# Polysketch attention into a SwiGLU block on one core: the first batch's third token block made of split products behind the first two blocks

## Chip, core and metric

One NeuronCore of a Trainium2 chip. The metric is device microseconds of one execution, from before the first instruction to after the last; three executions of the kernel before took 278.92, 278.66 and 278.62 us (median 278.66). The engines are TensorE (PE, with its weight loads, PEld), VectorE (DVE), ScalarE (ACT), GpSimd (POOL), and SyncE (SP), which issues the DMAs.

## What is computed

```python
# attention: batch 4, heads 4, 1088 tokens, head_dim 32, r = 8
def phi(x):
    a = np.einsum('rd,bhsd->bhsr', S1, x)
    b = np.einsum('rd,bhsd->bhsr', S2, x)
    return np.einsum('bhsi,bhsj->bhsij', a, b).reshape(*x.shape[:-1], r * r)
q_p, k_p = (phi(q), phi(k))
kv = np.einsum('bhsf,bhsd->bhfd', k_p, v)
z = np.sum(k_p, axis=2)
num = np.einsum('bhsf,bhfd->bhsd', q_p, kv)
den = np.einsum('bhsf,bhf->bhs', q_p, z)[..., None] + 1e-06
attn = num / den
# bridge: (B,H,S,D) -> (B*S, H*D), 4352 tokens of 128
x = np.ascontiguousarray(attn.transpose(0, 2, 1, 3)).reshape(B * S, H * D)
# d_model 128, d_ff 1536
g = x @ w_gate
silu = g * (1.0 / (1.0 + np.exp(-g)))
out = (silu * (x @ w_val)) @ w_out
```

Inputs and output are float32, except that S1, S2 and the three weights arrive as float64 words, which the kernel narrows to FP32 itself.

## The kernel before

**Blocks and units.** The 4352 tokens are ten blocks: batch 0 has blocks 0, 1 and 2 of 384, 384 and 320 tokens; from block 3 on (`HEAD`, the first of `line`) a block has 480 tokens, the last 384. d_ff is cut into 12 chunks of 128. A *unit* (i, j) makes hidden chunk j of block i: a gate and a value product with the 128 x 128 weights of chunk j, a SiLU on ScalarE, and a product of both on VectorE. A *down* (i, j) multiplies the hidden chunk by a 128 x 128 piece of w_out and accumulates in one PSUM bank per block; after a block's twelfth down, `store` transposes it on VectorE and SP writes it out with four or eight DMAs.

**Two kinds of products.** In blocks 0 to 2, `unit` (L1026) uses plain FP32 products (L1034). A plain FP32 product shows as two PE records. From block 3 on a unit is made of parts: `start_unit` (L990) multiplies a difference of the weights (wd) with a difference of the tokens (xd), L997, and ScalarE scales both PSUM banks in place (L1000); `finish_unit` (L1002) adds two products per bank on top, w1 by x1 (L1010) and wb by x0 (L1011); then SiLU (L1013) and a VectorE product (L1018). These six matmuls are of type fp32r and show as one record each. The tokens' parts x1, x0, xd are made by `cut_tokens` (L873), one ScalarE and two VectorE or POOL operations; the weights' parts w1, low, wb, wd by `cut_weights` (L840), for each of four groups of three chunks, in four steps: ScalarE, an engine for the subtraction, ScalarE, the engine again. Some downs of later blocks are made of parts too (L1074 to L1077).

**Banks.** PSUM has eight banks: g0, g1, g2, acc (0 to 3) and two pairs a (4, 5) and b (6, 7). A plain unit takes two of the first four in turn, a down's sum one of g1, g2, acc. `pair()` gives the least lately used free pair out of (0, 1), (4, 5) and (6, 7). A unit of parts holds its pair from its start until the VectorE product is recorded.

**Attention of the batches.** Batch 0 is done by itself at the beginning, block by block (`divide`, L539, writes the tokens xT). For the others a generator, `attentions()` (L615), is asked for its next piece by `parts_of(n)`: turning keys and queries on VectorE (L327, L578), key products (L354), key features (L377), their sums on POOL (`feature_sums`, L543), key-value products (L388), the spread of these by transposes and six small DMAs (`spread_out`), query sketches (L342), the query step (L745 to L762: a dot product, a sum, an addition, a reciprocal, a multiplication, and three times features and a transpose), and the numerators (L780), which ScalarE and VectorE copy into xT.

**The order.** It is written out by hand: each engine runs its instructions in the order in which the program records them. After the first units of blocks 0 and 1, the loop at L1300 runs over 30 plain units of blocks 0, 1 and 2; between them stand the narrowing of weights (`part`), the loads of batch 1, and from the 18th unit on one down per unit, a piece of attention, and the cutting of weights. The loop from L1345 then runs the downs that are left, three at a time, with pieces of attention between, until the numerators of batch 1 are done and block 3's tokens are cut; `start_unit(0)` and the last two downs follow. The main loop over the units of blocks 3 to 9 (L1376) starts the next unit, finishes this one, and makes a down when more than five are waiting.

Of the kernel before, what the change touches and what calls it, by code (L numbers as in the profile page):

```python
# [19 lines left out]
def kernel(  # L20
# [162 lines left out]
    coming += [("wo", i) for i in range(len(pieces["wo"]))]  # L183
# [126 lines left out]
    NH = 27  # L310
# [231 lines left out]

    def feature_sums(phk):  # L543

        rows = phk[:].rearrange("p c h i j -> p c (h i j)")
        s = apool.tile([P, 4, H * F], FP32, tag="zs", name="zs")
        add = lambda o, a, b: nc.gpsimd.tensor_tensor(out=o, in0=a, in1=b, op=ALU.add)

        def last():
            add(s[:, 0, :], s[:, 0, :], s[:, 1, :])  # L550
            add(s[:, 0, :], s[:, 0, :], rows[:, 8, :])

        return s[:, 0, :], [
            lambda: add(s[:, 0:2, :], rows[:, 0:2, :], rows[:, 4:6, :]),
            lambda: add(s[:, 2:4, :], rows[:, 2:4, :], rows[:, 6:8, :]),
            lambda: add(s[:, 0:2, :], s[:, 0:2, :], s[:, 2:4, :]),
            last,
        ]
# [56 lines left out]
    def attentions():  # L615
# [4 lines left out]
        yield from turn_queries(1)  # L620
        hold("a")
        kp = wide("a")
# [8 lines left out]
        for i, (c0, c1) in enumerate(kpieces):  # L631
            nc.scalar.copy(ka[:, H * c0 : H * c1, :], sketch(kp, i)[:, :, 0, :])
        phk = apool.tile([P, NC, H, R, R], FP32, tag="phk", name="phk")
        for n, (i, c0, c1) in enumerate(((0, 0, 3), (0, 3, 5), (1, 5, 7), (1, 7, 9))):
            first = H * (c0 - kpieces[i][0])
            kb = sketch(kp, i)[:, first : first + H * (c1 - c0), 1, :]
            key_features(phk, (ka[:, H * c0 : H * c1, :], kb), c0, c1)
            if n == 3:
                release("a")
            if n % 3 != 1:  # L640
                yield
        zs, sums = feature_sums(phk)
        for f in sums:
            f()
        yield from turn_keys(2)
        kvz = wide("a")
        key_values(kvz[:, 0, 0:F], phk, 0, NC)
        value_sums(kvz[:, 0, :], zs)
        kab, kcopies = sketched(wide("b"), key_products, 2, "kab2")
        fold(kvz[:, 0, :])  # L650
        spread = spread_out(1, kvz[:, 0, :])
        hold("a", "b")
        yield
        qab, copies = sketched(wide("a"), query_sketches, 3, "qab")
        run_copies(copies, 2)
        yield
        run_copies(kcopies, 2)
        release("a", "b")
# [3 lines left out]
        yield  # L662
        yield
        numerators(1, spread, (wide("a"), wide("b")))
# [159 lines left out]
    def homes(w):  # L824


        if w is wv:
            for c in range(4):
                yield [
                    stage.tile([P, 3, P], F32R, tag=tag, name=name, bufs=6)[:]  # L830
                    for tag, name in (("exp", "w1"), ("man", "wb"), (("exp", "man")[c % 2], "wd"))
                ]
        else:
            big = lambda pool, tag, bufs: pool.tile([P, 2, 3, P], F32R, tag=tag, name="g" + tag, bufs=bufs)
            for c in range(2):
                t = [big(stage, "raw", NRAW), big(stage, "raw", NRAW), big(apool, "phq", 2)]
                for k in range(2):
                    yield [x[:, k] for x in t]

    def cut_weights(w, lows, engine):  # L840

        rows = [], [], [], []
        sub = dict(op=ALU.subtract)
        for c, (w1, wb, wd) in enumerate(homes(w)):
            src = w[:, 3 * c : 3 * c + 3, :]
            low = lows[c]
            w_parts[id(w), c] = (w1, wb, wd)
            fine = dict(out=wd, in0=whole(w1), in1=whole(wb), **sub), engine.tensor_tensor
            if engine is nc.vector:
                fine = dict(  # L850
                    out=wd, in0=low, scalar=-BETA, in1=whole(w1), op0=ALU.mult, op1=ALU.add
                ), engine.scalar_tensor_tensor
            for row, f, args in zip(
                rows,
                (nc.scalar.activation, engine.tensor_tensor, nc.scalar.activation, fine[1]),
                (
                    dict(out=w1, in_=src, func=AF.Copy, scale=CUT),
                    dict(out=low, in0=src, in1=whole(w1), **sub),
                    dict(out=wb, in_=low, func=AF.Copy, scale=BETA),
                    fine[0],  # L860
                ),
            ):
                row.append((f, args))
        return rows

    def take(steps, n):

        for _ in range(n):
            if steps:
                f, args = steps.pop(0)  # L870
                f(**args)

    def cut_tokens(i, engine=nc.gpsimd):  # L873
# [21 lines left out]
        first, second = (difference, low) if engine is nc.vector else (low, difference)  # L895
# [94 lines left out]
    def start_unit(y):  # L990

        i, j = line[y // NCH], y % NCH
        n = blocks[i][1]
        xd = x_parts[i][2][:, 0:n]
        ps = sums_of[y] = pair(y)[:, :, 0:n]
# [6 lines left out]
    def finish_unit(y):  # L1002
        i, j = line[y // NCH], y % NCH
        n = blocks[i][1]
        x1, x0, _ = (x[:, 0:n] for x in x_parts[i])
        ps = sums_of.pop(y)
# [14 lines left out]
        let_go(y)  # L1021
# [4 lines left out]
    def unit(i, j, late=False, between=(None, None)):  # L1026
# [3 lines left out]
        g, u = bank(), bank()  # L1030
# [29 lines left out]

    def down(y=None):
# [3 lines left out]
        if j == 0:  # L1065
            acc[i] = bank("g1" if i == 1 else "g2" if i in line[2::2] else "acc")
# [3 lines left out]
        sides = dict(start=(j == 0), stop=(j == NCH - 1))  # L1070
# [12 lines left out]
        if i != LAST:  # L1083
            hidden.pop((i, j))
            slots.append(slot_of[i, j])
        if j == NCH - 1:
            if mine:
                put_together(y, i, n)
            else:
                store(i, n)  # L1090
# [153 lines left out]
    begun = [False]  # L1244

    def parts_of(n):

        for _ in range(n):
            if ahead[0] not in ("pe", "end"):
                ahead[0] = next(att, "end")  # L1250
                begun[0] |= ahead[0] == "first"
# [36 lines left out]

    w = ("wg", "wv")

    parts = {}
    for z, p in enumerate(both(3, *w) + both(4, *w) + [("wo", i) for i in range(4)]):
        z += z // 2 * 4
        for at in (z, z + 1, z + 2 + z % 6):
            parts.setdefault(at, []).append(p)
    seq = [(0, 3), (0, 4), (0, 5), (2, 0), (2, 1), (2, 2)]
    seq += [(i, j) for i in (1, 2) for j in range(3, 6)]
    seq += [(i, j) for j0 in (6, 9) for i in range(3) for j in range(j0, j0 + 3)]
    order = [(i, j) for i in range(3) for j in range(NCH)]
    for z, (i, j) in enumerate(seq):  # L1300
        if z == 17:
            free_banks.pop()
            turn[0] %= 4
        unit(i, j)
        for p in parts.get(z, ()):
            part(*p)
        if z in (24, 25, 26):
            catch_up()
        if z == 6:
# [3 lines left out]
        if z >= 17:  # L1313
            todo.remove(order[0])
            todo.insert(0, order.pop(0))
            down()
        if z == 20:
            lows = [
                pool.tile([P, 3, P], FP32, tag=tag, name="low", bufs=bufs)[:]
                for pool, tag, bufs in ((apool, "qb", 2), (apool, "dT", 2), (apool, "rd", 2), (apool, "qb", 2))  # L1320
            ]
            first, low, second, third = cut_weights(wv, lows, nc.gpsimd)
        if z in (20, 21):
            take(first, 2)
        if z == 21:
            take(low, 3)
# [110 lines left out]
```

## Time and profile before

| what | value |
|---|---|
| runs | 278.92, 278.66, 278.62 us; median 278.66 |
| the profiled execution, own time | 278.89 us |
| its span | 277.2 us, granted PE clock 1.00 |
| PE busy 26.7 to 49.2 us (plain units) | 22.50 of 22.50, DVE 19.46, ACT 13.43, POOL 8.19 |
| 49.2 to 77.0 (units, downs, attention of batch 1) | 27.80 of 27.80, DVE 21.29, ACT 14.70, POOL 18.64 |
| 77.0 to 91.4 (downs, query step, numerators) | 14.40 of 14.40, DVE 12.50, ACT 2.56, POOL 1.76 |
| L1034 at 384 columns | 96 records |
| L1034 at 320 columns | 48 records |
| L1082, downs before the main loop | 48 records at 384 columns, 24 at 320 |
| ACT scale L1000 | 958 ns at 960 columns, 795 at 768 |
| ACT SiLU at 320 columns, L1038 | 433 ns |
| DVE product at 320 columns, L1049 | 482 to 485 ns |
| POOL subtraction of 384 columns, L871 | 1001 ns (low), 1347 ns (wd) |

The span is what the profile sees of the program; the time of the execution has 1.7 us around it. A PE record's duration holds the pipe's drain, so neighbouring records overlap and the busy share says little; what counts is the distance from one start to the next.

### The profile page before, as it was taken

How to read it: one execution, taken by the hardware profiler on the slowest of the kernel's cores; microseconds unless marked ns; L12 is line 12 of the kernel's file. 1: busy time of each engine (PE TensorE's matmuls, PEld its weight loads, DVE VectorE, ACT ScalarE, POOL GpSimd, SP SyncE). 2: the span in 40 equal slices, each digit the busy share in tenths (PEclk: the TensorE clock that was granted, in tenths of full speed). 3: DMA queues.
4: the chain of work that ended last, by engine and by line, in shares of the span. 5: the costliest groups of instructions: out<-in, count | busy, mean ns of one | idle time of the engine just before them, and what ended most of it. 6: DMA issues, size and time to landing. Idle time of an engine off the chain costs nothing.

```text
span 277.2 us, 5670 instructions
## 1 busy us (share of the span) xinstructions
PE 271.4 (98%) x2169; PEld 198.3 (72%) x2169; DVE 203.7 (74%) x355; ACT 184.5 (67%) x330; POOL 98.9 (36%) x110
## 2 busy tenths in 40 slices
PE   8899999999999999999999999999999999999995
PEld 7645565666766787777577777867887888788994
DVE  3997987977688873887545766967877995987431
ACT  3468665565421586667479898769879878886860
POOL 3313422179820440060034353435425553542000
PEclk9999999999999999999999999999999999999999
DMA  6573195221151123000200020000100200010011
GB/s 192 168 220 79 54 277 185 74 89 57 39 114 28 26 85 94 2 1 0 38 13 4 0 39 0 0 2 10 27 0 2 36 0 1 9 29 0 10 29 28
DMA packets 26139, 14.30 MB, mean 52 GB/s; under 512 B 19840, under 2 KB 24192, under 8 KB 26112
## 3 DMA queue, kind: packets, MB, share of 16 engines
q1 hardware_dynamic: 25456, 13.84, 19.4%
q8 instruction: 17, 0.28, 0.4%
q10 hardware_dynamic: 656, 0.10, 0.2%
q14 instruction: 10, 0.08, 0.1%
HBM read 11.41 MB, written 2.23 MB: 49 GB/s over the span
## 4 chain that ended last, share of the span: by engine, by line
PE 94%; DVE 2%; DMA 2%; ACT 1%; issue 0%; SPq 0%
PE PS L1082 22%; PE PS L1034 16%; PE PS L1010 13%; PE PS L997 13%; PE PS L1011 13%; PE PS L1074 2%; PE PS L1077 2%; PE PS L1076 2%; PE PS L354 2%; PE PS L780 2%; PE PS L342 2%; PE PS L388 2%; DMA kld<-in_k_dram 2%; PE PS L1110 1%; PE PS L497 1%; PE PS L445 1%
## 5 line engine op out<-in xcount | busy, mean ns | idle before, releaser
L1000 ACT ACTIVATE PS<-PS 128x960 f32<-128x960 f32 (+1 forms) x84 | 78.5, 935 | 32.0 <-PE PS L997 31.2
L1018 DVE SCALAR_TENSOR_TENSOR hbuf<-PS,sg 128x480 f32<-128x480 f32 (+1 forms) x84 | 53.7, 640 | 43.6 <-ACT sg L1013 40.8
L1013 ACT ACTIVATE sg<-PS 128x480 f32<-128x480 f32 (+1 forms) x84 | 46.7, 556 | 2.0 <-PE PS L1011 1.2
L997 PE MATMUL PS<-xd,gphq 128*128 128x480 f32 (+1 forms) x84 | 47.3, 564 | 0.0
L1082 PE MATMUL PS<-hbuf,wo 128*128 128x480 f32 (+3 forms) x118 | 45.9, 492 | 0.0
L1010 PE MATMUL PS<-x,graw 128*128 128x480 f32 (+1 forms) x84 | 32.1, 382 | 0.0
L1011 PE MATMUL PS<-x,wb 128*128 128x480 f32 (+1 forms) x84 | 31.6, 376 | 0.0
L997 PE MATMUL PS<-xd,wd 128*128 128x480 f32 (+1 forms) x84 | 31.4, 374 | 0.0
L1010 PE MATMUL PS<-x,w 128*128 128x480 f32 (+1 forms) x84 | 31.4, 374 | 0.0
L1011 PE MATMUL PS<-x,graw 128*128 128x480 f32 (+1 forms) x84 | 31.3, 373 | 0.0
L1034 PE MATMUL PS<-xT,wg 128*128 128x384 f32 (+1 forms) x72 | 28.7, 480 | 0.0
L1034 PE MATMUL PS<-xT,wv 128*128 128x384 f32 (+1 forms) x72 | 28.0, 470 | 0.2 <-DVE wv L286 0.2
L1082 PEld LDWEIGHTS PS<-hbuf,wo 128*128 128x128 f32 x118 | 22.1, 189 | 7.4 <-issue 0.9
L1038 ACT ACTIVATE sg<-PS 128x384 f32<-128x384 f32 (+1 forms) x30 | 13.8, 465 | 18.8 <-PE PS L1034 17.2
L997 PEld LDWEIGHTS PS<-xd,gphq 128*128 128x128 f32 x84 | 15.8, 188 | 10.0 <-ACT PS L1000 6.4
L997 PEld LDWEIGHTS PS<-xd,wd 128*128 128x128 f32 x84 | 15.8, 189 | 9.9 <-issue 6.7
L884 POOL TENSOR_TENSOR x<-xT,x 128x480 fp32r<-128x480 f32 (+1 forms) x6 | 7.2, 1195 | 37.6 <-ACT x L881 37.6
L1034 PEld LDWEIGHTS PS<-xT,wv 128*128 128x128 f32 x72 | 13.4, 190 | 8.9 <-DVE hbuf L1049 0.9
L1034 PEld LDWEIGHTS PS<-xT,wg 128*128 128x128 f32 x72 | 12.9, 189 | 9.3 <-issue 1.2
L1010 PEld LDWEIGHTS PS<-x,graw 128*128 128x128 f32 x84 | 15.7, 187 | 3.5 <-ACT PS L1000 0.8
L1082 PE MATMUL PS<-hbuf,scaled 128*128 128x480 f32 x36 | 17.4, 565 | 0.0
L1010 PEld LDWEIGHTS PS<-x,w 128*128 128x128 f32 x84 | 15.8, 188 | 2.2
(184 smaller groups left out, 494.5 us busy)
## 6 DMA issues: line engine op xcount, KB each, us to landing
kld<-in_k_dram SPq DMA_DIRECT2D x4, 544.0 KB, 4.4
vld<-in_v_dram SPq DMA_DIRECT2D x12, 144.0 KB, 4.7
qld<-in_q_dram SPq DMA_DIRECT2D x3, 544.0 KB, 4.2
raw<-in_moe_w_out_dram SPq DMA_DIRECT2D x4, 384.0 KB, 4.0
raw<-in_moe_w_gate_dram SPq DMA_DIRECT2D x3, 384.0 KB, 3.6
raw<-in_moe_w_val_dram SPq DMA_DIRECT2D x3, 384.0 KB, 3.7
out_dram<-o SPq DMA_DIRECT2D x16, 60.0 KB, 2.0
vld<-in_v_dram SPq DMA_DIRECT2D x4, 112.0 KB, 4.3
```

Of the source, the lines that this page charges most:

```text
L342: nc.tensor.matmul(ps[32 * a : 32 * a + 32, 96 * (c - c0) : 96 * (c - c0) + 96], qT[:, 4 * c + a, :], s123[:, a : a + H, :, :].rearrange(" ...
L354: nc.tensor.matmul(ps[32 * a : 32 * a + 64, 64 * (c - c0) : 64 * (c - c0) + 64], kT[:, c, a : a + 2, :].rearrange("p a t -> p (a t)"), s12 ...
L884: engine.tensor_tensor(out=x0[:, 0:n], in0=x, in1=whole(x1[:, 0:n]), op=ALU.subtract)
L997: nc.tensor.matmul(ps[:, k], w_parts[id(w), j // 3][2][:, j % 3, :], xd, start=True, stop=True)
L1000: nc.scalar.activation(ps, ps, AF.Copy, scale=-1.0 / WHOLE)
L1010: nc.tensor.matmul(ps[:, k], w1, x1, start=False, stop=False, skip_group_check=True)
L1011: nc.tensor.matmul(ps[:, k], wb, x0, start=False, stop=True, skip_group_check=True)
L1013: nc.scalar.activation(sg, ps[:, 0], AF.Silu, scale=WHOLE)
L1018: nc.vector.scalar_tensor_tensor(out=hj[:, 0:n], in0=ps[:, 1], scalar=WHOLE, in1=sg, op0=ALU.mult, op1=ALU.mult)
L1034: nc.tensor.matmul(o[:, 0:n], w[:, j, :], xT[:, t0 : t0 + n], start=True, stop=True)
L1038: nc.scalar.activation(sg[:, 0:n], g[:, 0:n], AF.Silu)
L1082: nc.tensor.matmul(acc[i][:, 0:n], w, hidden[i, j][:, 0:n], **sides)
```

## The change

Blocks 0 and 1 alone are made of plain units. The loop over units has 18 steps in place of 30, all of 384 columns; no downs stand in it. Then come 20 downs in a row, then twelve units of block 2 made of parts, each with one down beside it. Into the downs and these twelve units go batch 1's attention, all cuts of weights (split by group into generators, `cut_weights`, driven by tables of steps), and the cut of block 2's tokens. The first wo piece is loaded last. Four downs of block 2 remain for the main loop. Key products, values and sketches of batch 1 take a pair from `pair()` in place of banks a and b. The sums of key features use three operations of 512 elements in another grouping. `start_unit` and `finish_unit` take (i, j); `down` takes its first and last by count; block 2's hidden chunks live in `late`.

```diff
-    coming += [("wo", i) for i in range(len(pieces["wo"]))]
+    coming += [("wo", i) for i in (1, 2, 3, 0)]
...
-            lambda: add(s[:, 0:2, :], rows[:, 0:2, :], rows[:, 4:6, :]),
-            lambda: add(s[:, 2:4, :], rows[:, 2:4, :], rows[:, 6:8, :]),
-            lambda: add(s[:, 0:2, :], s[:, 0:2, :], s[:, 2:4, :]),
+            lambda: add(s, rows[:, 0:2, :], rows[:, 2:4, :]),
+            lambda: add(s, s, rows[:, 4:6, :]),
+            lambda: add(s, s, rows[:, 6:8, :]),
...
-        yield from turn_queries(1)
-        hold("a")
-        kp = wide("a")
+        kp = pair("keys")
...
-        yield
-        yield
-        numerators(1, spread, (wide("a"), wide("b")))
+        numerators(1, spread)
...
+    def cut_weights(w, c, low, engine):
+
+        w1, wb, wd = w_parts[id(w), c] = home(w, c)
+        src = w[:, 3 * c : 3 * c + 3, :]
+        nc.scalar.activation(out=w1, in_=src, func=AF.Copy, scale=CUT)
+        yield
+        low = low[0]
+        engine.tensor_tensor(out=low, in0=src, in1=whole(w1), op=ALU.subtract)
+        yield
+        nc.scalar.activation(out=wb, in_=low, func=AF.Copy, scale=BETA)
+        yield
+        if engine is nc.vector:
+            nc.vector.scalar_tensor_tensor(
+                out=wd, in0=low, scalar=-BETA, in1=whole(w1), op0=ALU.mult, op1=ALU.add
+            )
...
+            engine.tensor_tensor(out=wd, in0=whole(w1), in1=whole(wb), op=ALU.subtract)
...
-    seq = [(0, 3), (0, 4), (0, 5), (2, 0), (2, 1), (2, 2)]
-    seq += [(i, j) for i in (1, 2) for j in range(3, 6)]
-    seq += [(i, j) for j0 in (6, 9) for i in range(3) for j in range(j0, j0 + 3)]
-    order = [(i, j) for i in range(3) for j in range(NCH)]
+    seq = [(i, j) for j0 in (3, 6, 9) for i in (0, 1) for j in range(j0, j0 + 3)]
     for z, (i, j) in enumerate(seq):
...
-        if z == 6:
+        if z == 8:
             load_k(1)
             load_v(1, [nc.sync] * 4)
             load_q(1)
...
+        if z >= 16:
+            parts_of(1)
...
+    order = seq + [(i, j) for i in (0, 1) for j in range(3)]
...
+    todo[:] = order
+    cuts = {"x": cut_tokens(2, soon=True)}
+    for c in range(4):
+        low = zlow if c == 3 else [free(late, NL - 3 + c)]
+        cuts["g%d" % c] = cut_weights(wg, c, low, nc.vector if c < 2 else nc.gpsimd)
+        cuts["v%d" % c] = cut_weights(wv, c, [free(room, 6 + c)], nc.gpsimd)
+    NB = 20
+    rest = {
+        1: ("v0", "v1"), 4: ("v0",), 5: ("g0",), 7: ("g0", "v2", "v3"), 9: ("g0", "v0"),
+        10: ("x",), 11: ("x", "g0", "v0"), 12: ("v1",), 14: ("g1",), 16: ("g1",),
+        17: ("g1", "v1"), 19: ("g1", "v1"),
+    }
+    for n in range(NB):
+        if n == NB - 2:
+            start_unit(2, 0)
+        down()
+        if n in (1, 2, 4):
+            part("wo", 0)
+        parts_of(n in (0, 2, 3, 5, 6, 8, 9, 15, 18))
+        at(cuts, *rest.get(n, ()))
+        if n in (12, 13, 14):
+            catch_up()
...
+    slots[:] = [late[:, c, :] for c in range(NL)]
+    rest = {
+        0: ("v2", "g2"), 1: ("g2", "g2", "v2"), 2: ("v2", "g2"), 3: ("g3", "v3"),
+        4: ("g3",), 5: ("g3", "v3"), 6: ("g3", "v3"),
+    }
+    for j in range(NCH):
+        ahead_first = j != 8
+        if not ahead_first:
+            parts_of(1)
+            x_steps = cut_tokens(HEAD, nc.vector, soon=True)
+        if not ahead_first:
+            finish_unit(2, j)
+        start_unit(*((2, j + 1) if j + 1 < NCH else (HEAD, 0)))
+        if ahead_first:
+            finish_unit(2, j)
+        down()
+        parts_of(j in (0, 2, 4, 6, 10, 11))
+        at(cuts, *rest.get(j, ()))
+        if j in (8, 9):
+            next(x_steps, None)
```

In the changed kernel's own line numbers the plain units' products are L1023, their VectorE products L1038, the downs L1076; a unit's parts are L987, the scale L990, L999 and L1000, SiLU L1002, the VectorE product L1007; the numerators are L783, the query step L748 to L765, the cuts of weights L850 to L862.

## What was forecast

> **What bounds the kernel now.** I read the page first: busy shares, then the chain that ended last.
>
> ```profile
> PE 271.4 (98%) x2169; PEld 198.3 (72%) x2169; DVE 203.7 (74%) x355; ACT 184.5 (67%) x330; POOL 98.9 (36%) x110
> PE 94%; DVE 2%; DMA 2%; ACT 1%; issue 0%; SPq 0%
> ```
>
> The chain runs through TensorE for 94% of the span: the time is the sum of what PE streams, plus its holes. A PE row's duration contains the drain of the pipe, so I take what one group adds to the chain of waits (start, us, what):
>
> ```profile
> 49.82 1.08 PE PS L1034 x4
> 54.34 0.65 PE PS L1082 x2
> 54.98 1.29 PE PS L1034 x4
> 77.00 9.89 PE PS L1082 x32
> 86.89 1.48 PE PS L780 x38
> ...
> 182.67 0.58 ACT sg L1013
> 183.27 0.67 DVE hbuf L1018
> 183.98 1.49 PE PS L780 x35
> ...
> 248.37 0.35 PE PS L997 x2
> ```
>
> A plain unit (two FP32 products, two records each) costs 1.08 us at 320 columns and 1.29 at 384; a down at 384 costs 0.65. Two products of parts (L997) cost 0.35 at 384 columns; at 480 they are pieces of 0.43 to 0.44. The 9.89 us at 77.00 is a stretch of downs that need nothing from VectorE, and behind it stand the numerators of batch 1 (L780). At 183 the numerators of batch 3 are held by an activation and a VectorE product: the only place of these lines where PE waits for others. The timeline of VectorE says what ran under the downs (start, us, engine, line, operation):
>
> ```profile
> 76.65 0.42 DVE L745 TENSOR_TENSOR dot<-qab 128x288 f32<-128x288 f32 x1
> 77.10 0.45 DVE L748 TENSOR_REDUCE den<-dot 128x36 f32<-128x288 f32 x1
> 77.59 0.18 DVE L750 TENSOR_SCALAR den<-den 128x36 f32<-128x36 f32 x1
> 77.81 0.38 DVE L751 RECIPROCAL den<-den 128x36 f32<-128x36 f32 x1
> 78.22 0.46 DVE L752 TENSOR_TENSOR qab<-qab,den 128x288 f32<-128x288 f32 x1
> ...
> 80.46 0.95 DVE L377 TENSOR_TENSOR phq<-qab 128x768 f32<-128x768 f32 x1
> 81.52 0.98 DVE L762 STREAM_TRANSPOSE phT<-phq 128x768 f32<-128x768 f32 x1
> ```
>
> That is the query step of batch 1, ending with the third transpose at 86.51; the numerators' weight loads begin at 86.82. So a VectorE chain of 9.9 us fits the 9.9 us of downs with nothing to spare.
>
> **The change, part by part.**
>
> *Block 2 by parts.* Removed: 12 units of 1.08 us. Added: 12 units of six fp32r products at 320 columns. No row has that width; 384 columns step at 0.35 / 2 = 0.175, 480 at 0.435 / 2 = 0.2175, so a straight line gives 0.147 and a unit 0.88. Gain 12 x (1.08 - 0.88) = 2.4 us. Bounds: if each step were held for the 0.187 us that a weight load shows, a unit is 1.12 and the change loses 0.5; in proportion to columns (0.175 x 320 / 384 = 0.146) it gains 2.5. Weight loads of 0.187 did not stop steps of 0.175, and the 128-column products of L1110 step at 1.80 / 16 = 0.11 with one load each, so I take 2.4.
>
> *Downs and units in another order.* 36 downs and 24 units of 384 columns stay at their prices; four downs of block 2 (0.54 each) slide into the first units of the main loop. These units are paced nearly as much by ScalarE (scale 0.87 and SiLU 0.48 from start to start, 1.35, against 6 x 0.2175 = 1.31), so the downs get perhaps 0.1 of the four's 2.15 us free. Two steps of 0.1 us at 32.85 and 33.53, where narrowing weights meets 320-column units, go: 0.2. Together 0.3 gained.
>
> *ScalarE.* 12 scale passes of 640 columns are new. Rows: 0.958 at 960, 0.795 at 768, so 0.69 on a line, 0.60 from start to start; SiLU 0.43, 0.37 from start to start. With cuts of 0.42 each, ScalarE has 8 x 0.97 + 6 x 0.42 = 10.3 us in the first eight units of block 2, where PE has 4 x (0.88 + 0.65) + 4 x (0.88 + 0.54) = 11.8. It fits: 0. If a cut has to wait for POOL, the scales queued behind it are late, and PE's next four products with them; that is a rival.
>
> *VectorE, where I see the price.* In the loop over block 2 the order is: product of unit 0, store of block 0, the five operations above, products 1 and 2, features and transpose, product 3, store of block 1, product 4, features and transpose, products 5 and 6, features and transpose, product 7; and then, ahead of unit 8, the numerators. They need the last transpose, and with unit 8 holding one of the three pairs of banks they take the pairs of units 6 and 7, so they need product 7 too. From start to start: products 8 x 0.40 (the 320-column product of L1049 at 72.10 lets the next begin at 72.50); stores 2 x 0.50; the query operations 76.65 to 78.59, 1.94; features and transposes 3 x 1.95. Sum 3.2 + 1.0 + 1.94 + 5.85 = 12.0 us. The first product can't start before its SiLU, which in ScalarE's order stands behind the scale of unit 1: 0.30 (start of unit 1) + 0.16 (drain) + 0.60 + 0.43 = 1.5 us into the loop. VectorE has idled till then, with the queries' copies ready. So the numerators start 13.5 us into the loop, PE is there after 11.8: a hole of 1.7. A part may show earlier, as starts of units 4 and 8 that wait for products 1 and 5; the sum is the same. Queued behind on PE: the end of unit 8, starts 9 and 10, all downs.
>
> *The cuts beside it.* Eight POOL operations (low and difference of the last two thirds of both weights) now run in the same 13 us; before, one did:
>
> ```profile
> 80.51 1.76 POOL L871 TENSOR_TENSOR wd<-w,wb 128x384 fp32r<-128x384 f32 x1 [5.24 <-ACT wb L871]
> 117.82 1.17 DVE L377 TENSOR_TENSOR late<-kab 128x512 f32<-128x512 f32 x1
> 173.75 1.99 DVE L377 TENSOR_TENSOR phq<-qab 128x768 f32<-128x768 f32 x1
> ```
>
> Beside a POOL operation, a VectorE one with both inputs in SBUF is stretched or stretches POOL: 1.17 where 0.68 is usual, 1.99 for 0.95, the dot 0.73 and 1.21 for 0.42, the 36-column addition 0.61 and 0.94 for 0.18; in the first line POOL took 1.76 for 1.0. Nine meetings, two of which cost VectorE nothing, add 4.0 us: 0.44 each. Of six exposed operations (dot, addition, multiplication, three features) I take three as meeting one: 1.3 us. Bounds: 0, and the largest seen of each, 0.80 + 0.75 + 0.18 + 3 x 1.04 = 4.8, against which stands that POOL has 8 us of cuts in 13.
>
> The Trainium skill (SBUF — State Buffer, "Who interferes with whom") states that a VectorE instruction with two SBUF inputs and a GpSimd one that reads SBUF exclude each other for the whole instruction, and that the order of issue decides who waits. It speaks against this change. By it each meeting could cost up to a POOL operation of 1.0 us, so six would make an estimated 6 us; the rows above show both orders and less.
>
> *After the numerators.* 1.44 us of PE as at 136.95 to 138.39. Start 9 then needs the first pair copied out: at 185.42 to 186.23 both ScalarE copies end 0.81 after the last product; PE covers 4 x 0.147 = 0.59 and needs a little to begin: 0.3 hole. In the kernel before, downs covered this.
>
> *At nothing.* Loads of batch 1 go from the seventh to the ninth unit, 8 units (10 us) ahead of their turn; landing takes 4.4. The first third of w_out is loaded last, after the three it passed on SP; it has ten units of time. Three of POOL's catch-up products move behind downs 13 to 15, and their downs come five or more downs (3 us) later. The sums for keys have the same five POOL operations, under downs 5 to 15, and are wanted after both products of batch 2's keys. The six spread transfers (about 0.55 each to issue) and four loads of v have eight units. Block 0's store waits on SP behind them, and nothing waits for it. Uncovered, the dearest of these, a late load, would cost its 4.4 landing.
>
> **Sum.** -2.4 - 0.3 + 1.7 + 1.3 + 0.3 = +0.6 us. Span 277.2 to 277.8; the profiled execution took 278.89, 1.7 more than its span, and the median of the runs is 278.66, so I forecast 279.3. A difference under 0.2% (0.56 us) can't be told from none.
>
> **Rivals.**
> - *Holes without POOL's share.* POOL's operations fall beside transposes and PSUM products, which didn't stretch. -2.4 - 0.3 + 2.0 = -0.7: 278.0. For it: two of nine meetings cost nothing. Against: cuts fill 8 of POOL's 13 us.
> - *Nearly the whole gain.* PE is so late at unit 8 for other reasons, or VectorE so early, that only the copy's 0.3 shows: -2.4: 276.3. Against: 12.0 us of VectorE rows against 11.8 of PE, and a start at 1.5.
> - *ScalarE held by POOL*, on the slow side. At units 1 and 5 it takes cuts whose POOL operation was issued one unit before; a POOL operation of 1.76 in place of 1.0 blocks scales 3 and 7. It decides once POOL is over 0.7 us late, PE's slack there (1.44 a unit less 0.16, 0.60 and a little). Two holes of about 0.8 on top of the forecast: +2.2, 280.9. For it: the 1.76 row; against: PE is late there anyway.
> - *Weight-load bound.* A unit is 0.24 dearer than on the line; the first eight units' 1.9 is hidden in the hole that VectorE makes, the last four add 1.0: 280.3. Against it the 0.175 steps.
>
> **Numbers.** Forecast 0.43, no POOL share 0.27, whole gain 0.08, ScalarE held 0.18, weight loads 0.04. Below -0.56: the whole gain, 0.15 of the second, 0.03 of the forecast, 0.26; within: 0.12 of the second and 0.14 of the forecast, 0.26; above: the rest, 0.48. The range 277.6 to 281.0 leaves out the whole gain, the weight loads and tails. The likeliest case alone: 278.6 to 280.2.
>
> **What would show it.** Steps of 0.147 for L987, L999 and L1000 at 320 columns. Numerators at L783 whose weight loads sit idle until the product of unit 7 (L1007), over 1 us, with VectorE busy from the first product to there. Features (L377) of over 0.95 beside POOL. Wrong if VectorE has holes in that stretch, if PE's wait at the numerators is under half a microsecond, or if the first waits of PE there are for scales (L990).

## The result, and the profile after

The changed kernel took 283.23 us (median of 4 runs, 282.45 to 283.38) beside 278.79 us of the kernel before (278.62 to 279.01): ratio 1.0153, 95% interval 1.0132 to 1.0174. It is slower, by 4.4 us (1.5%); the forecast was 279.3 with an upper bound of 281.0. The profiled execution of the changed kernel took 283.08 us with a span of 281.4, against 278.89 and 277.2, so 4.2 us more span is to be explained.

The page after, in the two lines that answer to the first two of the prediction (busy times; the chain that ended last, by engine):

```profile
PE 270.4 (96%) x2193; PEld 199.9 (71%) x2193; DVE 207.7 (74%) x352; ACT 192.6 (68%) x343; POOL 105.2 (37%) x115
PE 80%; DVE 10%; ACT 3%; issue 3%; DMA 2%; SPq 1%; DVEq 0%
```

TensorE had 94% of the chain and has 80%; VectorE went from 2% to 10%. Where it entered, the chain of waits of the changed kernel tells (start, us, what):

```profile
53.51 0.63 DVE kT L327
54.18 0.69 PE PS L354 x16
54.86 9.87 PE PS L1076 x30
...
84.15 0.49 DVE late L1007
84.64 1.00 DVE phq L377
85.67 0.99 DVE phT L765
86.80 1.77 PE PS L783 x41
```

Before, 9.89 us of downs led straight into the numerators, with no other engine between. Now a product, a feature piece and a transpose of VectorE lead into them, and a turn of keys into the key products. TensorE's groups between 26.8 and 93 us, with the idle time just before them and what ended it, name every place (line, operation, count | busy, mean ns | idle, releaser):

```profile
L1023 PE MATMUL PS<-xT,wv 128*128 128x384 f32 x36 | 14.9, 495 | 1.0 <-POOL wv L286 0.8 <-DVE hbuf L1038 0.2
L987 PE MATMUL PS<-xd,wd 128*128 128x320 f32 x12 | 3.9, 323 | 1.0 <-DVE late L1007 1.0
L354 PE MATMUL PS<-s,kT 128*64 128x64 f32 x72 | 2.8, 226 | 0.9 <-DVE kT L327 0.9
L783 PE MATMUL PS<-phT,spread 32*32 32x288 f32 (+1 forms) x64 | 1.8, 398 | 1.5 <-DVE phT L765 1.5
```

Four waits: a narrowed third of w_val, the turned keys, a product of block 2, and the numerators' last transpose. The kernel before shows none of over 0.1 us between 26 and 125 us. A record of L1023 lasts 0.49 us while the next one starts 0.32 us behind it, so the idle time shown is about 0.16 us short of what each wait costs by starts. The runs below are told in idle time as shown, the account of the prediction behind them by starts. The third and fourth were in the prediction. The first two were not.

The first, in the timeline of the changed kernel (start, us, engine, line, operation):

```profile
33.21 1.00 POOL L286 TENSOR_TENSOR wg<-man,exp 128x384 f32<-128x384 f32 x1 [3.26 <-DVE man L277]
33.51 1.11 DVE L271 SCALAR_TENSOR_TENSOR exp<-raw,exp 128x384 int32<-128x384 int32 x1
35.17 1.00 POOL L286 TENSOR_TENSOR wv<-man,exp 128x384 f32<-128x384 f32 x1 [0.96 <-DVE man L277]
36.22 0.91 PE L1023 MATMUL PS<-xT,wv 128*128 128x384 f32 x2 [0.80 <-POOL wv L286]
```

The third of w_val for chunk 6 is ready at 36.17 and wanted by the seventh unit of the loop at about 35.27. In the kernel before it was ready at 36.12, no earlier, but six units of block 2 stood ahead of chunk 6 as well, so it was first used by the thirteenth. VectorE was also held: its narrowing operation (L271, 0.55 us alone) took 1.11 beside GpSimd.

In block 2's loop, VectorE of the changed kernel:

```profile
73.60 0.49 DVE L1007 SCALAR_TENSOR_TENSOR late<-PS,sg 128x320 f32<-128x320 f32 x1 [2.24 <-ACT sg L1002]
...
74.51 0.93 DVE L748 TENSOR_TENSOR dot<-qab 128x288 f32<-128x288 f32 x1
...
76.58 0.89 DVE L755 TENSOR_TENSOR qab<-qab,den 128x288 f32<-128x288 f32 x1
...
84.15 0.49 DVE L1007 SCALAR_TENSOR_TENSOR late<-PS,sg 128x320 f32<-128x320 f32 x1 [0.43 <-ACT sg L1002]
84.56 1.08 DVE L377 TENSOR_TENSOR phq<-qab 128x768 f32<-128x768 f32 x1
85.67 0.98 DVE L765 STREAM_TRANSPOSE phT<-phq 128x768 f32<-128x768 f32 x1
```

The loop began at 71.75. VectorE idled 2.24 us until the first SiLU, as foreseen, and then was busy but for 0.43 us to the last transpose. The numerators started at 86.80, 15.05 us into the loop.

### The profile page after: what moved, and what is told of

Read it like the earlier page. It is cut to its first block, busy times and chain, and to the rows that moved or that the text cites. A ratio compares the mean times of both kernels' runs of the same rounds, so it can differ in the third digit from the quotient of the medians.

```text
span 281.4 us, 5759 instructions
## 1 busy us (share of the span) xinstructions
PE 270.4 (96%) x2193; PEld 199.9 (71%) x2193; DVE 207.7 (74%) x352; ACT 192.6 (68%) x343; POOL 105.2 (37%) x115
## 4 chain that ended last, share of the span: by engine, by line
PE 80%; DVE 10%; ACT 3%; issue 3%; DMA 2%; SPq 1%; DVEq 0%
PE PS L1076 19%; PE PS L999 14%; PE PS L987 14%; PE PS L1000 13%; PE PS L1023 3%; PE PS L1068 2%; PE PS L1071 2%; PE PS L1070 2%; PE PS L783 2%; PE PS L354 2%; PE PS L388 2%; DMA kld<-in_k_dram 2%; DVE man L277 1%; DVE hbuf L1038 1%; PE PS L342 1%
## 5 line engine op out<-in xcount | busy, mean ns | idle before, releaser
L990 ACT ACTIVATE PS<-PS 128x960 f32<-128x960 f32 (+2 forms) x96 | 86.8, 904 | 33.9 <-PE PS L987 32.7
L1007 DVE SCALAR_TENSOR_TENSOR hbuf<-PS,sg 128x480 f32<-128x480 f32 (+1 forms) x84 | 53.7, 639 | 43.4 <-ACT sg L1002 40.5
L1002 ACT ACTIVATE sg<-PS 128x480 f32<-128x480 f32 (+2 forms) x96 | 51.9, 541 | 2.0 <-PE PS L1000 1.3
L1076 PE MATMUL PS<-hbuf,wo 128*128 128x480 f32 (+2 forms) x106 | 42.1, 500 | 0.0
L987 PE MATMUL PS<-xd,graw 128*128 128x480 f32 (+2 forms) x72 | 40.5, 563 | 0.1
L987 PE MATMUL PS<-xd,wd 128*128 128x480 f32 (+2 forms) x96 | 35.3, 367 | 1.0 <-DVE late L1007 1.0
L999 PE MATMUL PS<-x,w 128*128 128x480 f32 (+2 forms) x96 | 35.1, 366 | 0.2 <-issue 0.2
L1000 PE MATMUL PS<-x,wb 128*128 128x480 f32 (+2 forms) x96 | 35.2, 366 | 0.0
L987 PEld LDWEIGHTS PS<-xd,wd 128*128 128x128 f32 x96 | 18.1, 189 | 12.4 <-issue 6.0
L1000 PE MATMUL PS<-x,graw 128*128 128x480 f32 (+2 forms) x72 | 26.3, 366 | 0.0
L1076 PEld LDWEIGHTS PS<-hbuf,wo 128*128 128x128 f32 x106 | 19.4, 189 | 5.2 <-issue 0.4
L1023 PE MATMUL PS<-xT,wv 128*128 128x384 f32 x48 | 19.8, 494 | 1.2 <-POOL wv L286 0.8
L1023 PE MATMUL PS<-xT,wg 128*128 128x384 f32 x48 | 19.8, 495 | 0.0
L1000 PEld LDWEIGHTS PS<-x,wb 128*128 128x128 f32 x96 | 18.0, 188 | 2.5 <-issue 0.4
L987 PEld LDWEIGHTS PS<-xd,graw 128*128 128x128 f32 x72 | 13.6, 188 | 8.5 <-ACT PS L990 4.1
L999 PEld LDWEIGHTS PS<-x,w 128*128 128x128 f32 x96 | 18.0, 188 | 2.2
L999 PE MATMUL PS<-x,graw 128*128 128x480 f32 (+2 forms) x48 | 18.2, 378 | 0.0
L999 PE MATMUL PS<-x,gphq 128*128 128x480 f32 (+2 forms) x48 | 17.7, 370 | 0.0
L1076 PE MATMUL PS<-hbuf,scaled 128*128 128x480 f32 x36 | 17.4, 564 | 0.0
L1023 PEld LDWEIGHTS PS<-xT,wv 128*128 128x128 f32 x48 | 8.8, 189 | 8.6 <-POOL wv L286 1.4
```

The source lines that it names most:

```text
L987: nc.tensor.matmul(ps[:, k], w_parts[id(w), j // 3][2][:, j % 3, :], xd, start=True, stop=True)
L990: nc.scalar.activation(ps, ps, AF.Copy, scale=-1.0 / WHOLE)
L999: nc.tensor.matmul(ps[:, k], w1, x1, start=False, stop=False, skip_group_check=True)
L1000: nc.tensor.matmul(ps[:, k], wb, x0, start=False, stop=True, skip_group_check=True)
L1002: nc.scalar.activation(sg, ps[:, 0], AF.Silu, scale=WHOLE)
L1007: nc.vector.scalar_tensor_tensor(out=hj[:, 0:n], in0=ps[:, 1], scalar=WHOLE, in1=sg, op0=ALU.mult, op1=ALU.mult)
```

## The experiments

Times are medians; the kernel before lay at 278.8 to 279.0 beside each of them. The changed kernel's 283.2 is what a single move is held against.

**Block 2's division later.**

```diff
-    divide(0, *steps[2], nd)
+    hold("a")
...
+        if n == 8:
+            divide(0, *steps[2], nd)
+            release("a")
```

> One part moved: block 2's division (VectorE, about 2.4 us ahead of the loop of plain units) is put behind the eighth down of the loop of downs; its PSUM bank is kept until then. Theory (the 18 plain units wait for weights narrowed late because VectorE, busy 23.28 of 24.90 us there, comes late to its narrowings and products): the holes of 0.95 us at the first unit of chunk 6 and of 0.34 us at a unit near 41.8 go, and part or all of the 1.15 us before the second batch's key products, together 1.3 to 2.4 us less than the 283.2 of the changed kernel: 280.8 to 281.9. Rival (the weights' transfers or GpSimd's own narrowing of 1.0 us are what is late): the holes stay and the time is 283.0 to 283.4.

282.91 us, ratio 1.0132 [1.0099, 1.0164]. The wait for w_val shrank from 0.80 to 0.48 us of idle, the other holes stayed. The 0.3 us is no more than single runs of one kernel differ by, so the time misses the theory's range; VectorE's load ahead of the loop is at most a small part of the cause.

**Key products two downs later.**

```diff
-        parts_of(n in (0, 2, 3, 5, 6, 8, 9, 15, 18))
+        parts_of(n in (2, 3, 4, 5, 6, 8, 9, 15, 18))
```

> One part moved: the second batch's key products are issued two downs later (behind the fourth and fifth down in place of the second and third), with nothing else taken away. Theory (the keys' turn on VectorE is late against the first downs, and the two holes of 0.76 and 0.39 us before the key products are lost on the path): the holes close and the time falls by about 1.1 us, to 282.1. Rival (VectorE is late by its load, so a later place only lets the next step of the attention be late, or the block-2 loop takes it back): within 0.3 us of 283.2.

281.91 us, 1.0093 [1.0061, 1.0125]: 1.3 less. In its timeline the 36 key products are one stretch with no wait before it:

```profile
53.66 1.27 PE L354 MATMUL PS<-s,kT 128*64 128x64 f32 x36
```

Nothing later in the loop of downs gave it back. A later place for the key products was enough, with VectorE's work as it was.

**Query step half a step earlier.**

```diff
-        parts_of(n in (0, 2, 3, 5, 6, 8, 9, 15, 18))
+        parts_of(n in (0, 2, 3, 5, 6, 8, 9, 15, 18, 19))
...
-        parts_of(j in (0, 2, 4, 6, 10, 11))
+        parts_of(j in (1, 3, 5, 10, 11))
```

> One part moved: the second batch's query step on VectorE begins one half-step earlier, at the end of the loop of downs, ahead of block 2's first product, and its later halves come one unit earlier; the numerators stay behind the same unit. Theory (the VectorE chain of block 2's loop is what ends last, and its 2.24 us idle before the first product could hold the first half of the step): the holes of 1.0 us at unit 4 and of 1.48 us at the numerators shrink, 1.5 to 2.5 us less than 283.2: 280.7 to 281.7. Rival (ScalarE's copies and SiLUs, or GpSimd's cuts of the weights, set the pace of this loop): at most 0.5 us less, 282.7 to 283.4.

282.74 us, 1.0129 [1.0084, 1.0175]. The holes of 1.01 at unit 4 and of 1.48 at the numerators went, but two others opened and only 0.5 us arrived, which four runs from 282.33 to 283.81 hardly tell from none: VectorE's second cut of w_gate now stood behind the query step and held the start of unit 3 (0.74), a product held a later start (0.53), and the numerators took 2.02 us in place of 1.72, since their weight loads waited 0.4 us for a scale and 0.3 for a product of the last unit, whose banks were not free. The time lies in the rival's range, but at both holes TensorE waits for VectorE, and not for ScalarE or GpSimd as the rival had it.

**GpSimd writes zeros in place of half of the cuts.**

```diff
+        if c > 1:
+            engine.memset(low, 0.0)
+        else:
             engine.tensor_tensor(out=low, in0=src, in1=whole(w1), op=ALU.subtract)
```

The same stands at the third part, wd.

> Leaves out the differences of the last two groups of w_gate's and w_val's parts (chunks 6 to 11): their tiles are filled with zeros by GpSimd, which then writes without reading, so the products of parts with them add nothing. Everything else is as in the changed kernel. Theory of the prediction (meetings of GpSimd with VectorE stretch VectorE's operations in block 2's loop by 0.44 us each, 1.3 us in all): the numerators come 0.9 to 1.5 us earlier, 281.7 to 282.3 us. Rival (the chain there is long by its operations alone, and no meeting counts): within 0.3 us of 283.2.

282.12 us, 1.0103 [1.0069, 1.0136]: 1.1 less. The dot product took 0.42 in place of 0.93 and the multiplication 0.46 in place of 0.89; the addition that follows still met the fills and took more than its 0.18:

```profile
75.13 0.64 DVE L753 TENSOR_SCALAR den<-den 128x36 f32<-128x36 f32 x1
```

The theory's range; the prediction's 1.3 us for GpSimd was right in size.

**Block 2 plain again, in the changed order.** In the loop over block 2, `start_unit` and `finish_unit` give way to one line:

```diff
+        unit(2, j, apart=True)
```

> One part undone: block 2's twelve units are plain products again (FP32, 1.08 us on TensorE by the kernel before, in place of 0.88), in the changed order, with the cuts of weights and tokens left where they are. Theory (VectorE's chain of query step, products and store turns sets when the numerators come, so TensorE's gain ahead of them only widens a hole): the eight units ahead of the numerators cost nothing more, the four behind them 4 x 0.2 = 0.8 us less the small holes there, so 283.3 to 284.1. Rival (the parts' gain of 12 x 0.2 = 2.45 us is in the time, and all the loss is elsewhere): 285.4 to 285.9.

283.34 us, 1.0146 [1.0106, 1.0186]. Undoing the parts cost 0.1 us, with single runs from 282.68 to 284.37: the theory's range, at its lower edge, and far from the rival's 285.4. Up to the first product of 480 columns TensorE is busy 64.14 us in place of 62.13 and idle 1.7 us less, and that product comes 0.3 us later. Little of the parts' gain was on the path.

**Numerators one unit later.**

```diff
-        ahead_first = j != 8
+        ahead_first = j != 9
...
-        if j in (8, 9):
+        if j in (9, 10):
```

> One part moved: the second batch's numerators stand behind unit 9's place and not unit 8's, with the third block's tokens cut one unit later. Theory (the hole of 1.48 us ahead of the numerators is VectorE arriving late, and 1.4 us of products of unit and down fit into it): 1.0 to 1.4 us less than 283.2, 281.8 to 282.2. Rival (the numerators' copies and the cuts of the next block's tokens follow them, so a later place delays the main loop's first unit by as much): 282.9 to 283.4.

282.31 us, 1.0110 [1.0074, 1.0146]: 0.9 less, just short of the theory's range; the hole before the numerators is gone.

**Narrowing earlier.**

```diff
-    divide(0, *steps[2], nd)
+    part("wg", 3)
+    part("wv", 3)
+    hold("a")
...
-        for t in (0, 1, 2):
-            parts.setdefault(z + t, []).append(p)
+        for t in ((0, z + 1) if p[1] == 3 and p[0] != "wo" else (z, z + 1, z + 2)):
+            parts.setdefault(t, []).append(p)
```

The division stands behind the eighth down, as in the first run.

> Block 2's division behind the eighth down as in the first run, and in its old place the first narrowing step of the fourth thirds of w_gate and w_val, each step of which so comes one to two units earlier. Theory (in the loop of plain units the first use of a narrowed third is too close behind its narrowing; in the first run VectorE still waited with it for its place among the units' products): the holes of 0.95 and 0.34 us go, 0.9 to 1.3 us less than 283.2: 281.9 to 282.3. Rival (VectorE is loaded to the end of this loop, so the stall only moves to the next products or the keys' turn): 282.7 to 283.2, as in the first run (282.9).

282.15 us, 1.0098 [1.0069, 1.0128]: 1.1 less, inside the theory's range. The seventh unit no longer waits for its third of w_val and the second hole is gone; a wait of 0.29 for a VectorE product stands before the sixth. The keys' holes stayed. Of the 1.1 us the division's later place alone had won 0.3; the greater distance from narrowing to use adds 0.8.

**All moves together.** The edits of the last run, the keys, the query step and the numerators.

> All moves together: division and narrowing as in the run before this one, key products two downs later, the query step half a step earlier, the numerators one unit later. Nothing is left out. Theory (the four losses are separate waits on the path of TensorE): 283.2 less 1.3 for the keys, 1.0 for the narrowing, 0.5 for the query step and 1.0 for the numerators, 279.4, from 278.8 to 280.1, still not below the kernel before. Rival (they are one shortage of VectorE, which the loop of block 2 pays for whichever hole is closed ahead): 280.6 to 281.6.

281.16 us, 1.0071 [1.0047, 1.0095]. Of 3.8 us that the four single runs won, 2.1 arrived. The rival's range: a hole of 0.95 us opened at unit 3, before a cut of w_gate on VectorE.

**Narrowing spaced apart from GpSimd.**

```diff
+    when = ((0, 1, 2), (1, 2, 4), (4, 5, 7), (7, 8, 9), (9, 10, 12), (12, 13, 14), (13, 14, 15))
```

Each third is narrowed at these three units of the loop, in place of three in a row; where two thirds meet at a unit, the later one goes first.

> Only the units at which the seven thirds of weights are narrowed in the loop of plain units are changed, so that GpSimd's multiplication of a third stands beside a unit's product and not beside the next third's narrowing on VectorE; every operation stays. In the changed kernel five narrowing operations of VectorE in this loop overlap GpSimd by 0.69 us and take 0.90 to 1.11 us in place of 0.35 and 0.55, 2.8 us in all, against 0.23 us of one in the kernel before. Theory (these meetings make VectorE, 22.3 us of work without them, longer than the 23.2 us of the loop's products, so they are the cause of its holes and of part of the late keys' turn): two short meetings stay, the holes of the loop go, 1.0 to 2.3 us less than 283.2: 280.9 to 282.2. Rival (VectorE's load and order in this loop decide with or without the meetings): 282.8 to 283.4.

283.90 us, 1.0174 [1.0159, 1.0189]: 0.7 worse, against both expectations. Three of the five stretched operations went, VectorE's busy time from 26.8 to 51.7 us fell from 23.28 to 20.93, and the second hole, the one that ended on a product, went with them. But the third of w_val had its last step one unit later:

```profile
35.57 0.99 POOL L286 TENSOR_TENSOR wv<-man,exp 128x384 f32<-128x384 f32 x1 [1.52 <-DVE man L277]
36.61 0.59 PE L1023 MATMUL PS<-xT,wv 128*128 128x384 f32 x1 [1.35 <-POOL wv L286]
```

TensorE idles 1.35 in place of 0.80. Here VectorE had time enough, and the distance between a narrowing and its use decided: one unit (1.29 us) later in the order cost 0.55, less than the unit, since the operation that had been stretched now took 0.55 and not 1.11. Over the whole loop this and the second hole left 0.3 us more than in the changed kernel. The larger loss came behind it: the last narrowing of w_out still met GpSimd (1.10 us), the turn of the keys began 1.2 us behind the first down in place of 0.5, and the idle time before the key products grew from 0.60 to 1.27. So distance and meetings both count; the run does not rule VectorE's load out.

**That spacing with the other moves.** The edits of the keys, query step and numerators, and the last cut of w_gate's second third one down earlier.

> That spacing together with the key products two downs later, the query step half a step earlier, the last VectorE cut of the second third of w_gate one down earlier, and the numerators one unit later; the division stays ahead of the loop. Nothing is left out. Theory (three shortages of VectorE on TensorE's path, of which spacing, keys and numerators each close one): from 279.6 to 280.8, below the 281.2 of the first version with all moves and above the 279.0 of the kernel before. Rival (block 2's loop alone, short of VectorE by its own work, takes back what is won ahead of it): 281.0 to 281.8.

281.95 us, 1.0102 [1.0085, 1.0119]: outside both. The first hole, 1.33, is that of the run before; where the first version with all moves waited 0.95 at unit 3 for the cut, 0.17 is left, which ends on a VectorE product.

**The best with parts.** All moves with the earlier narrowing, and this cut:

```diff
-        17: ("g1", "v1"), 19: ("g1", "v1"),
+        17: ("g1", "v1"), 18: ("g1",), 19: ("v1",),
```

> All moves of the first version with all moves, and the last VectorE cut of the second third of w_gate one down earlier, so that the query step does not stand in front of it. Nothing is left out. Theory (in that version unit 3 waited 0.95 us for this cut, and 0.18 us with the earlier place): 0.5 to 1.0 us below its 281.2, so 280.2 to 280.7, still above the kernel before at 279.0, since VectorE holds the loop of block 2 at three smaller places. Rival (what is closed at this unit opens at a later one): 281.0 to 281.4.

280.23 us, 1.0040 [1.0022, 1.0059]; the theory. Three holes of 0.25 to 0.33 us are left in block 2's loop, each ahead of a matmul that waits for a product on VectorE. The last of them stands behind a feature piece that took 1.62 us in place of 0.93, beside two cuts of GpSimd:

```profile
80.49 1.62 DVE L377 TENSOR_TENSOR phq<-qab 128x768 f32<-128x768 f32 x1
83.65 0.39 PE L987 MATMUL PS<-xd,wd 128*128 128x320 f32 x1 [0.33 <-DVE late L1007]
```

**The same with plain units.** `unit(2, j, apart=True)` again.

> The run before it with block 2's twelve units as plain FP32 products again. Theory (with the other moves VectorE no longer decides everywhere in block 2's loop, so here, other than in the changed kernel where undoing the parts cost 0.1 us, part of the parts' 2.4 us is in the time): 0.6 to 1.6 us above the run before it. Rival (the parts are still hidden behind VectorE): within 0.4 us of it. A second rival (the parts pay in full): 2.2 us or more above it.

279.44 us, 1.0011 [0.9995, 1.0026]: 0.8 *below* the version with parts, outside all three expectations. By its interval, which goes by means, it is level with the kernel before; by medians it is 0.6 us above it. The same 15 us of both versions, with parts and then plain (window, length, busy us of PE, PEld, DVE, ACT, POOL):

```profile
70.50:85.50 15.00, 14.17 (x76) 10.71 (x74) 13.28 (x22) 11.74 (x24) 10.80 (x10) 1.00 0.32 67
```

```profile
70.50:85.50 15.00, 15.00 (x101) 10.02 (x113) 13.29 (x22) 6.23 (x15) 10.51 (x9) 1.00 0.32 67
```

VectorE does the same work, but with plain units TensorE never waits. What took the parts' gain was left to two explanations: GpSimd's stretch, or the parts' own hold of bank pairs.

**Zeros again, with all moves.** The edit of the run with zeros, in the version with parts:

> The version with all moves and the earlier cut (280.2 us), in which the differences of the last two groups of w_gate's and w_val's parts (chunks 6 to 11) are left out: GpSimd fills their tiles with zeros, so it writes without reading. Theory A (the parts lose in block 2's loop because GpSimd stretches VectorE's features from 0.93 to as much as 1.62 us): the three small holes of 0.25 to 0.33 us before unit starts go, and 0.7 to 1.2 us with them, 279.0 to 279.5. Theory B (the parts' own hold of PSUM pairs and the numerators' wait for a pair, 2.03 us in place of 1.50, decide): at most 0.5 us, 279.7 to 280.2.

280.42 us, 1.0042 [1.0017, 1.0067], single runs from 278.66 to 283.28. The profiled execution (282.02 us) shows a wait that this edit itself made:

```profile
71.28 3.25 DVE L753 TENSOR_SCALAR den<-den 128x36 f32<-128x36 f32 x1
...
71.56 0.42 POOL L854 MEMSET room<- 128x384 f32 x1
...
74.08 0.41 POOL L865 MEMSET wd<- 128x384 f32 x1
...
75.98 0.38 PE L992 MATMUL PS<-xd,wd 128*128 128x320 f32 x1 [2.79 <-DVE late L1012]
```

An addition over 36 columns (0.38 in the version without zeros) lasted from 71.28 to 74.53; the last of eight zero fills in a row ended at 74.49. Inconclusive.

And in the version with plain units:

> The same edit and the same part left out, in the version with all moves and block 2's units plain (279.4 us). Both theories: TensorE has no hole in block 2's loop there, so a quicker VectorE wins nothing, 279.2 to 279.6. Then by theory A the version with parts comes to within 0.3 us of this one or below it; by theory B it stays 0.4 us or more above.

279.66 us, 1.0024 [1.0006, 1.0041], no hole in block 2's loop; as both theories had it (the time is 0.06 us above their range), so it tells only that TensorE binds there.

**No GpSimd cuts of the last two groups.**

```diff
+        low = src if c > 1 else low[0]
+        if c > 1:
+            w_parts[id(w), c] = w1, wb, w_parts[id(w), 1][2]
+        else:
             engine.tensor_tensor(out=low, in0=src, in1=whole(w1), op=ALU.subtract)
```

The subtraction for wd is also only done for the first two groups.

> The version with all moves and the earlier cut (280.2 us), in which GpSimd's eight operations on the last two groups of w_gate's and w_val's parts are left out: the second part of these groups (chunks 6 to 11) is scaled from the whole weight, and the third is that of chunks 3 to 5. ScalarE's cuts and all of TensorE's products stay. Theory A (the parts lose in block 2's loop because GpSimd stretches VectorE's features): the features take 0.93 us, the holes of 0.25 to 0.33 us before unit starts go, 0.7 to 1.3 us less, 278.9 to 279.5. Theory B (the parts' own hold of PSUM pairs decides): at most 0.4 us less, 279.8 to 280.2, with the holes in place.

278.75 us, 0.9996 [0.9979, 1.0014]: 1.5 below the version with parts and a little below theory A's range. No hole of over 0.08 us is left in the loop. The edit takes away GpSimd's stretch of VectorE and also every wait for these cuts themselves; but the three holes of the version with parts all ended on VectorE's products. Its features, and those of the version with these cuts (line, operation | busy, mean ns):

```profile
L377 DVE TENSOR_TENSOR phq<-qab 128x768 f32<-128x768 f32 x3 | 2.8, 933 | 0.0
```

```profile
L377 DVE TENSOR_TENSOR phq<-qab 128x768 f32<-128x768 f32 x3 | 3.7, 1219 | 0.0
```

And with plain units:

> The same edit and the same part left out with block 2's units plain (279.4 us). Both theories: there is no hole in block 2's loop there for a quicker VectorE to close, 279.2 to 279.5. By theory A the parts are then level with plain units or better by up to 0.6 us, by theory B still worse by 0.4 us or more.

279.60 us, 1.0028 [1.0014, 1.0043], 0.1 above the range of both theories. Without these cuts the parts are 0.85 us better than plain units; with them 0.8 worse. Theory A: GpSimd's cuts beside VectorE's query step take 1.65 of the 2.45 us that the parts save on TensorE. The numerators' longer time with parts stays: from the down before them to the next it is 3.92 us against 3.31 with plain units, where the unit between is 0.2 shorter. In the run without these cuts the numerators' weight loads wait 0.4 us for a scale and 0.4 for a product of the unit before, and with plain units for neither, so banks have a share too. That this costs the other 0.8 us was not tried.

## Why the prediction was wrong

Right in sign, 3.9 us short of the time. By its steps:

- *Block 2 by parts, -2.4.* The steps were right: 0.145 to 0.147 us at 320 columns, so 12 x (1.077 - 6 x 0.1455) = 2.45 us of TensorE work. No weight-load bound. The sum put all of it down as won and took back 1.6 of it, of the eight units ahead of the numerators, inside the holes. Of the other 0.8, of the four units behind them, the run that undid the parts shows 0.1, with single runs 1.7 us apart.
- *Downs and units in another order, -0.3: the step that failed.* "36 downs and 24 units of 384 columns stay at their prices" did not hold. The loop of 18 plain units lost 0.95 + 0.34 + 0.1 = 1.4 us to narrowed weights and products, of which an earlier narrowing, together with a later division, won 1.1. The prediction looked at who reads a third, but not at how many units stand between its last narrowing step and its first use: two, where there had been seven. Nor did it count that VectorE's narrowing meets GpSimd in this loop (0.55 us became 1.11).
- *At nothing: failed for the keys' turn.* Loads landed in time, as said. The key products themselves stood behind the first down, where VectorE was still turning keys: 0.76 + 0.39 = 1.15 us, and 1.3 by the run. "8 units (10 us) ahead of their turn" was counted for the transfer, never for the VectorE step behind it.
- *ScalarE, 0.* Held. No hole of TensorE in this loop ends on a scale, and the rival with ScalarE held by GpSimd did not occur. VectorE, though, idled 0.43 us for a SiLU at 84.15, a hole in the stretch that the prediction wanted without one.
- *VectorE's chain, +1.7 and GpSimd's share, +1.3.* The mechanism was right: the wait at unit 4 for product 1 and at the numerators for the last transpose. They did not need product 7 first: it ended at 87.02, they began at 86.80. Forecast 14.8 us from the loop's start to the numerators, measured 15.05; the first product came 1.85 us into the loop, not 1.5, since the scale of unit 1 began 0.79 us into it and not 0.46. GpSimd's share was 1.1 by the run with zeros. The rows beside GpSimd were the dot, the multiplication and one feature, 0.51 + 0.43 + 0.13 = 1.07 us. The Trainium skill ("SBUF — State Buffer", section "Who interferes with whom") has a VectorE instruction with two SBUF inputs and a GpSimd one that reads SBUF exclude each other, by the estimate in the prediction for 6 us. The trace shows the stretch at a fifth of that.
- *After the numerators, +0.3 and 1.44.* The numerators took 1.72 us, start 9 lost 0.37, and the end of unit 9, not in the sum, 0.27: 0.6 more.
- *Main loop.* From the first 480-column product to the end 188.12 us in place of 185.76, so 2.36 more where the four downs less 0.1 were put at 2.05.

Sum of what was missed: 1.4 + 1.15 + 0.25 + 0.6 + 0.3 = 3.7, less 0.05 of the parts, on the forecast's 0.6: 4.3, against 4.2 measured. The two unforeseen waits make 2.55 of it, and the runs that closed each (1.1 and 1.3) bear that out. Without them the sum comes to 1.7 us more than the kernel before, 280.4: still slower, and inside the range.

The whole comes to this: from 26.7 us to the first product of 480 columns the kernel before had 53.3 us of VectorE work in 64.7 us, in an order in which TensorE shows no wait of 0.1 us. The changed kernel has 55.4 us in 66.6, in an order that makes TensorE wait at four places. No version tried with the complete computation was faster than the kernel before; the best of them, 0.6 us above it by medians, uses no parts in block 2. Whether another spread of GpSimd's cuts keeps the parts' gain stays open.

## What to carry to other kernels

When the order of units changes, count for each prepared operand the units between its preparation and its first use, in both kernels, engine by engine, before calling any unit's price unchanged. A saving on the bounding engine counts only where that engine is still the last to arrive: price the loop as the larger of the two engines' sums.

## What was not expected of the hardware

Single-input VectorE work suffered beside GpSimd as well: a mask of 384 columns (L263, a TENSOR_SCALAR with one SBUF input) took 0.90 us in place of 0.35 with 0.69 us of overlap. The prediction's rows had it already in the 36-column addition (0.61 and 0.94 for 0.18), which it put among operations with both inputs in SBUF though it has one. The section of the Trainium skill named above lists tensor_scalar among the operations that can take both ports, so it agrees. And eight short zero fills in a row, each of 0.41 to 0.43 us and reading nothing, held one addition on VectorE (also a TENSOR_SCALAR) for 3.25 us, to the end of the whole row. In the changed kernel's order the same eight fills stood in a row too, but the addition began near its end: it took 0.64 us, to 75.77, where the last fill ended at 75.74. The dot product beside the same fills kept its 0.42 us.
